# A spectral-filter and gated-MLP block, forward and backward: shift term at frequency 0, a written order of the opening's loads, sums by ones columns, and the last tile from PSUM

## Chip, cores, metric

The kernel runs on one core of one Trainium2 chip. The metric is the device time of one execution in microseconds (us); the time of a kernel is the median of its runs. Beside the runs there is one profiled execution of the same program, whose trace is read here.

## What is computed

The reference is one transformer-like block over x of 2048 rows (S) and 576 columns (D), and the gradients of all its inputs for a given grad_out:

```python
mod = silu(c) @ w_mod                       # six rows of 576: sa, ca, ga, sb, cb, gb
h = layernorm(x) * (1 + ca) + sa
x1 = x + ga * irfft2(rfft2(h) * (w_r + 1j * w_i))
h2 = layernorm(x1) * (1 + cb) + sb
out = x1 + gb * ((h2 @ w_gate) * (h2 @ w_up)) @ w_down
```

w_gate and w_up are 576 x 4608, w_down is 4608 x 576, w_mod is 576 x 3456, c is one row. All inputs are bf16. The outputs are out_0 (the block's result) and the gradients of x (out_1), w_r and w_i (out_2, out_3), w_gate, w_up, w_down (out_4 to out_6), c (out_7) and w_mod (out_8).

## The kernel before, in words

Rows go in 16 tiles (NT) of 128. D is padded to 640 (DP) where five blocks of 128 are wanted. The stages in order of time, in the profile's microseconds:

- **Opening and s1, 0 to about 60.** On SP, one load after the other: x in pieces (`x_load`), the three thirds of w_mod that are wanted first (`mod_load` of MCA, MSA, MGB), the row table RD, the column table G1, grad_out in three pieces (gonA, gonB, gonC). PE runs useless matmuls ("warm", L305) until the first data is there. `scaled_table` (L367) makes the columns of ca with 25 tiny matmuls (`mod_cols`, "modc") and scales the table RD by 1 + ca into RDs (L373, all five slabs on DVE). `shift_rows` (L376) does the same 25 matmuls for sa, puts the result into two columns of msl (L379), multiplies with RD ("zms", L384) and writes the product's row, split in a high and a low bf16 part, into two spare rows of RDs (L385 to L387). The padding of the normed tiles n1r holds ones in the columns that meet these rows (L283), so that the row transform adds sa's transform to every row. Then `pipeline` runs three steps over the tiles: `s1_norm` (statistics by `s1_stats`, normalisation on ACT, L429, transposes "trp", L434), `s1_cols` (row transform "zp", L443, with RDs; evacuation "zt") and `s1_rows` (column step "vp", L462 and L463, with G1). Statistics are made for 1, 3, 4, 4 and 4 tiles at once. Loads from x(4:8) on wait for a DVE instruction of `scaled_table` (`issue_after(first)`). `mod_make` stores each modulation row to modb_d from SP (L340).
- **u4, s2, s3, to about 300.** Transposes of grad_out (goT, L489) and products with w_down (u4, L517) fill PE. s2 takes 19 chunks of frequencies: second column step, spectrum Xc copied by ACT, stored to xn_d, multiplied with the filter ("fm", L235), first inverse step. s3 is the inverse transform, x1, the second layernorm (n2, stored to n2_d) and h2.
- **Main loop, about 300 to 1255**: 36 blocks of 128 columns of the MLP, forward and backward.
- **Tail, 1255 to the end.** t1 (per tile: the backward of the second layernorm, sums for the modulation's gradients, first steps of the transform of the gradient), t2 (filter backward, in chunks), t3 (inverse transform, backward of the first layernorm by `norm_back`, sums, store of out_1). The down projection for out_0 (u3, L1350) is dealt out between these as filler: a fixed number of its matmuls stands in PE's order after each step, and what is left follows after t3.

The sums: a column sum over rows of gh is a product with a ones pattern (`colsum`, L971; two matmuls of 288 columns per tile and sum), and the sum over rows of gh * n is taken from the diagonals of five matmuls (`diag`, L974; 4 of 128 columns and one of 64). All of a stage's tiles add up in one PSUM bank or two, opened and closed by products with zeros (`add_zero`, L966, 512 columns each). `diag_rows` (L981) masks the diagonal on DVE, `of_rows` and `of_sums` turn the sums into rows with 288-column fp32 matmuls ("spp", L991), and `section` (L1000) copies them (dmb, L1003, two buffers), writes one sixth of out_8 and adds to out_7 by products on DVE ("pr", L1016). `filter_grad` (L1188, "gwt") makes the gradients of the filter, whose spectrum Xn it loads on POOL; `store_grads` (L1322) writes them from POOL. The last half tile of out_0 goes from PSUM by ACT to a bf16 tile (L1353), then on DVE a product with gb (L1360) and a sum with x1 (L1361), then a store from POOL (L1362).

What sets the order: a scheduler orders each engine's instructions when the program is built; `in_order(list)` pins the order of the instructions given, `issue_after` and `behind` put a wait or an order behind others, `pipeline` interleaves the steps of successive tiles. At run time each engine works through its own order and waits at the first instruction that isn't ready. SP and POOL issue DMA in such an order too.

Of the kernel before, what the change touches and what calls it, by code (L numbers as in the profile page):

```python
# [9 lines left out]
FP32 = mybir.dt.float32  # L10
# [12 lines left out]
DP = 640  # L23
DF = 289
# [74 lines left out]
def build(ctx, tc, A_x, A_w_r, A_w_i, B_w_gate, B_w_up, B_w_down, c_in, w_mod, grad_out,  # L99
# [27 lines left out]
    n2_d = dram("n2_d", [128, NT, D], BF)  # L127
# [14 lines left out]
    pick = glob.tile([128, 2, 128], BF, name="pick")  # L142
    nc.vector.memset(pick[:], 0.0)
    for q in range(2):
        nc.vector.memset(pick[:, q, 64 * q:64 * q + 64], 1.0)


# [114 lines left out]
    with ExitStack() as hs:  # L262
# [18 lines left out]
        for n_ in n1r:  # L281
            nc.gpsimd.memset(n_[:, :, D:DP], 0.0)
            nc.gpsimd.memset(n_[:, :, D:DP:32], 1.0)  # L283
        RDs = hw2.tile([128, 5, 2, FP], BF, name="RDs", bufs=1)
        nc.gpsimd.memset(RDs[64:128, 4], 0.0)
        msl = hw2.tile([128, 5, 128], BF, name="msl", bufs=1)
# [9 lines left out]

        with tc.high_priority(60), nc.allow_non_contiguous_dma(reason="tiny c load"):
            c_bf = hp1.tile([128, 5], BF, name="c_bf")
            nc.vector.memset(c_bf[:], 0.0)
            nc.sync.dma_start(c_bf[:, 0:4], c_in[0, 0:512].rearrange("(m q) -> q m", q=128))  # L300
            nc.sync.dma_start(c_bf[64:128, 4:5], c_in[0, 512:576].rearrange("(m q) -> q m", q=64))
# [26 lines left out]
        def mod_make(j, wm, eng="v"):  # L328
# [11 lines left out]
            return nc.sync.dma_start(modb_d[:, j, :], modh[j][:]).ins  # L340
# [12 lines left out]
        wms = {}  # L353
        x_load(0, 1)
        wms[MCA] = mod_load(MCA)
        wms[MSA] = mod_load(MSA)
        T = {"RD": load_table(hp1, "RD", "tA")}
        x_load(1, 4)
        T["G1"] = hp1.tile(TABS["G1"], BF, name="T_G1", tag="tB")

        def g1_load(t0, t1):
            nc.sync.dma_start(T["G1"][:, t0:t1].rearrange("p a b c -> p (a b c)"), tab_d["G1"][:, t0 * 384:t1 * 384])

        g1_load(0, 4)
        opca_c = hp1.tile([128, 5], FP32, name="opca_c")

        def scaled_table():  # L367
# [3 lines left out]
            for m in range(5):  # L371
                r = slice(0, min(128, D - 128 * m))
                nc.vector.tensor_scalar(out=RDs[r, m].rearrange("p c f -> p (c f)"), in0=T["RD"][r, m].rearrange("p c f -> p (c f)"), scalar1=opca_c[r, m:m + 1], scalar2=None, op0=MUL)  # L373
            return one.ins

        def shift_rows():  # L376
            ps, parts = mod_cols(wms[MSA])
            for r, k in parts:
                nc.vector.tensor_copy(msl[r, k, 64:128:32], ps[r, k].unsqueeze(2).to_broadcast([r.stop, k.stop - k.start, 2]))  # L379
            hi = hp1.tile([128, 2, FP], BF, name="hi")  # L380
            for cc in range(2):
# [3 lines left out]
                nc.scalar.copy(RDs[64:65, 4, cc, :], zp[64:65, :FP])  # L385
                nc.vector.tensor_copy(hi[96:97, cc, :], zp[96:97, :FP])
                nc.vector.tensor_tensor(out=RDs[96:97, 4, cc, :], in0=zp[96:97, :FP], in1=hi[96:97, cc, :], op=SUB)  # L387
# [3 lines left out]
        def s1_stats(t):  # L391
            n = 1 if t == 0 else 4 - t % 4
# [14 lines left out]
        with tc.issue_after(first):  # L407
            x_load(4, 8)
            g1_load(4, NT)
            wms[MGB] = mod_load(MGB)  # L410
            for t0, t1, g in gons:
                nc.sync.dma_start(g[:, 0:(t1 - t0) * D].rearrange("p (t d) -> p t d", d=D), go_v[:, t0:t1, :])
            x_load(8, 12)
            T["BD2"] = load_table(hp1, "BD2")
            T["BDA"] = load_table(hp1, "BDA")

# [4 lines left out]
        def s1_norm(t):  # L421
            c4, tt = t // 4, t % 4
            if t == 4:
                with tc.issue_after(first):
                    x_load(12, NT)
            if tt == (1 if c4 == 0 else 0):
                s1_stats(t)
# [40 lines left out]
        mark1 = traced()  # L468
        shift_rows()
        dve0 += on_dve(mark1)[0:2]  # L470
# [4 lines left out]
        in_order(dve0 + on_dve(mark)[0:9])  # L475
# [4 lines left out]
        with tc.issue_after(first):  # L480
            nc.sync.dma_start(wn[:, 0, :, 0:DF], wr_v)
            nc.sync.dma_start(wn[:, 1, :, 0:DF], wi_v)
# [8 lines left out]
        FB4 = 2  # L491
        TWICE = 20
        turns, stored, wdTs, sts, u4_done, u4r = [], [], {}, {}, [0], []

        def u4_group(g, eng=None):
            fb, sb4 = g // 4, g % 4
            k, j = fb // FB4, fb % FB4
            if g % (4 * FB4) == 0:
                wdTs[k] = (u4w if not u4r or k % 5 < 2 else u4r[0]).tile([128, FB4, 5, 128], BF, name="wdT")
                wdn = wdn2[:, k % 2, :, :]  # L500
                with tc.issue_after(first):
                    rows = B_w_down[fb * 128:(fb + FB4) * 128, :].rearrange("(j f) d -> f j d", f=128)
                    nc.sync.dma_start(wdn[:, :, 0:D], rows)
                    nc.sync.dma_start(wdn[:, :, D:DP], rows[:, :, 512:D])
                turns.append(nc.sync.dma_start_transpose(out=wdTs[k][:].rearrange("q j m f -> q (j m) f"), in_=wdn.rearrange("f j d -> f (j d)")).ins)
# [24 lines left out]
        with ExitStack() as rc:  # L530
# [16 lines left out]
            def s2_filter(ci):  # L547
# [4 lines left out]
                X = c2.tile([128, 2, NT, 16], BF, name="Xc", bufs=3)  # L552
                if ng < 4:
                    nc.gpsimd.memset(X[:], 0.0)
                evac(X[:].rearrange("k c a m -> k (c a) m")[:, :, 0:w].rearrange("k e (j f) -> k j e f", f=4), xp[:, 0:ng, :].rearrange("k j (e f) -> k j e f", f=4), eng="a")
                nc.sync.dma_start(xn_d[:, ci * 512:(ci + 1) * 512], X[:].rearrange("k c a f -> k (c a f)"))
# [42 lines left out]

        uts, ybs, h2_made = {}, {}, []  # L600
# [19 lines left out]
        def s3_norm(sa):  # L620
# [5 lines left out]
            n2 = hw2.tile([128, 2, D], BF, name="n2")  # L626
# [6 lines left out]
            for i in range(2):  # L633
                nc.scalar.activation(out=n2[:, i, :], in_=x1[:, i, :], func=ACT.Identity, bias=nmr2[:, i:i + 1], scale=rstd2g[:, s0 + i:s0 + i + 1])
                nm = hw2.tile([128, D], BF, name="nm")
                nc.vector.tensor_tensor(out=nm[:], in0=n2[:, i, :], in1=modh[MCB][:], op=MUL)
# [238 lines left out]
    with ExitStack() as ts:  # L875
# [44 lines left out]
        sel = tl.tile([128, 2, 128], FP32, name="sel")  # L920
# [11 lines left out]
        def norm_back(pool, gn, n, rstd, res, out, name):  # L932
# [4 lines left out]
            nc.vector.scalar_tensor_tensor(out=w[:], in0=gn[:], scalar=rstd, in1=n, op0=MUL, op1=MUL, accum_out=s12[:, 1:2])  # L937
# [3 lines left out]
            if name == "1":  # L941
                nc.scalar.activation(out=w[:], in_=n, func=ACT.Identity, bias=ab[:, 0:1], scale=ab[:, 1:2])
            else:
                nc.vector.tensor_scalar(out=w[:], in0=n, scalar1=ab[:, 1:2], scalar2=ab[:, 0:1], op0=MUL, op1=ADD)
# [21 lines left out]
        def add_zero(*banks, first):  # L966

            for cs in banks:
                nc.tensor.matmul(cs[:], lhsT=ident[:], rhs=zero[:], start=first, stop=not first)

        def colsum(cs, h, src):  # L971
            nc.tensor.matmul(cs[:, 0:288], lhsT=pick[:, h, :], rhs=src, start=False, stop=False)

        def diag(cs, cs4, off, a, b):  # L974

            for m in range(5):
                o = cs[:, wide(m)] if m < 4 else cs4[:, off:off + 64]
                w = 128 if m < 4 else 64
                nc.tensor.matmul(o, lhsT=a[:, wide(m)] if m < 4 else a[:, D - 128:D], rhs=b[:, m * 128:m * 128 + w], start=False, stop=False)

        def diag_rows(pool, cs, cs4, off, name):  # L981
# [462 lines left out]
```

## Time and profile before

| | |
|---|---|
| median of 3 runs | 1522.07 us (1521.61 to 1528.6) |
| profiled execution | 1523.45 us |
| its span in the trace | 1521.7 us |
| PE busy | 1495.4 us (98%) |
| DVE busy | 1048.5 us (69%) |
| ACT busy | 580.3 us (38%) |
| POOL busy | 241.0 us (16%) |
| mean granted PE clock | 0.993 |

Engines: PE is the matmul engine (TensorE; PEld its weight loads), DVE the vector engine, ACT the scalar engine, POOL is GpSimd, SP is SyncE, which here only issues DMA (SPq is its queue). In the timeline a row is: start, duration, engine, line, operation, output<-input, shape, count, and in brackets the idle time just before it with the instruction or DMA that ended that time. Durations of matmuls overlap, so their pace is read from the starts. In groups, the columns behind the bar are total busy time, mean in ns, and idle time before with its main cause. In the windows, each engine's busy time is followed by the granted PE clock, the share of the DMA engines' time and GB/s.

### The profile page before, as it was taken

To read this page: it belongs to the slowest core of one execution; us is meant where nothing else is said; L and a number is where in the kernel's file an instruction comes from. 1 tells how busy PE (TensorE), PEld (TensorE's weight loads), DVE (VectorE), ACT (ScalarE), POOL (GpSimd) and SP (SyncE) were. 2 spreads that over 40 slices of the span, in tenths; PEclk is the share of its full clock that TensorE was granted. 3 is DMA by queue.
4 is the path that set the end of the run, shared out by engine and by line. 5 is a ranking of instruction groups with operands and counts; after the bars stand their busy time and mean duration, and the time that the engine had idled before them with its cause. 6 is when DMAs were issued, how large, how long until landed. Compare 5 with 4: busy or idle time off the path is not lost. (4 is left out here: it accounts for less than half of the span.)

```text
span 1521.7 us, 29239 instructions
## 1 busy us (share of the span) xinstructions
PE 1495.4 (98%) x11260; PEld 1020.0 (67%) x11264; DVE 1048.5 (69%) x2620; ACT 580.3 (38%) x1182; POOL 241.0 (16%) x368
## 2 busy tenths in 40 slices
PE   7999999999999999999999999999999999999998
PEld 5666643566667666666676666666766767788866
DVE  6666843667767667677676676776776777688884
ACT  5767842322222222222222222222222226586763
POOL 1101212101111111111120110110210113221022
PEclk8999999999999999999999999999999999999999
DMA  9988996688868679578688587677777779965687
GB/s 315 277 227 222 270 255 202 148 164 164 170 122 176 141 128 192 119 151 157 136 156 164 126 164 147 143 158 141 155 146 140 151 180 241 298 212 185 186 286 198
DMA packets 489470, 278.26 MB, mean 183 GB/s; under 512 B 410769, under 2 KB 461074, under 8 KB 488306
## 3 DMA queue, kind: packets, MB, share of 16 engines
q1 hardware_dynamic: 461170, 173.14, 53.5%
q0 software_dynamic: 28160, 103.25, 23.0%
q8 instruction: 88, 1.44, 0.4%
q14 instruction: 52, 0.43, 0.1%
HBM read 106.59 MB, written 82.16 MB: 124 GB/s over the span
## 5 line engine op out<-in xcount | busy, mean ns | idle before, releaser
L816 DVE TENSOR_TENSOR acc<-acc,u8p 128x288 f32<-128x288 f32 (+1 forms) x1088 | 482.9, 452 | 276.2 <-PE u8p L811 272.7
L811 PE MATMUL u8p<-wT,ggT 128*128 128x288 bf16 x1152 | 327.9, 286 | 1.6 <-DVE acc L816 1.6
L811 PE MATMUL u8p<-wT,guT 128*128 128x288 bf16 x1152 | 327.6, 286 | 0.0
L775 PE MATMUL gup<-h2T,wgu 128*128 128x512 bf16 x1152 | 297.8, 379 | 0.0
L710 ACT CAST so<-u57p 128x288 bf16<-128x288 f32 x216 | 86.2, 399 | 532.6 <-PE u57p L708 527.3
L708 PE MATMUL u57p<-h2p,gu_sf 128*128 128x288 bf16 x1152 | 186.4, 286 | 0.0
L708 PE MATMUL u57p<-h2p,gg_sf 128*128 128x288 bf16 x1152 | 185.9, 286 | 0.0
L775 PEld LDWEIGHTS <-wgu 128*128 128x128 bf16 x1152 | 109.6, 98 | 97.9 <-issue 16.6
L811 PEld LDWEIGHTS <-ggT 128*128 128x128 bf16 x1152 | 112.6, 98 | 66.5 <-issue 14.0
L517 PE MATMUL u4p<-goT,wdT 128*128 128x512 bf16 x656 | 151.9, 379 | 0.0
L811 PEld LDWEIGHTS <-guT 128*128 128x128 bf16 x1152 | 112.7, 98 | 57.6 <-issue 2.4
L1350 PE MATMUL u3p<-wd,hl 128*128 128x288 bf16 x936 | 142.4, 289 | 0.0
L777 ACT CAST gT<-gup 128x512 bf16<-128x512 f32 x144 | 84.4, 586 | 131.8 <-PE gup L775 129.9
L708 PEld LDWEIGHTS <-hh_sf 128*128 128x128 bf16 x1152 | 112.7, 98 | 28.4
L708 PEld LDWEIGHTS <-gu_sf 128*128 128x128 bf16 x1152 | 112.4, 98 | 28.5
L708 PEld LDWEIGHTS <-gg_sf 128*128 128x128 bf16 x1152 | 112.4, 98 | 28.2
L1350 PEld LDWEIGHTS <-hl 128*128 128x128 bf16 x1152 | 108.4, 99 | 26.0 <-issue 0.3
L777 ACT CAST uT<-gup 128x512 bf16<-128x512 f32 x144 | 84.4, 586 | 77.5 <-PE gup L775 77.5
L517 PEld LDWEIGHTS <-wdT 128*128 128x128 bf16 x656 | 61.3, 98 | 71.1 <-issue 7.3
L708 PE MATMUL u57p<-gonC,hh_sf 128*128 128x288 bf16 x576 | 99.7, 286 | 0.0
L788 POOL DMA_DIRECT2D hhT_d<-hhT x36 | 33.3, 925 | 376.3 <-DVE hhT L779 333.5
L173 DVE CAST ghh_st<-u4p 128x512 bf16<-128x512 f32 x56 | 38.6, 690 | 58.7 <-PE u4p L517 57.3
(389 smaller groups left out, 1864.9 us busy)
## 6 DMA issues: line engine op xcount, KB each, us to landing
ghhT_d<-ghh_st POOLq DMA_DIRECT2D x36, 512.0 KB, 4.3
ghh<-ghhT_d POOLq DMA_DIRECT2D x36, 512.0 KB, 7.7
hhT_d<-hhT POOLq DMA_DIRECT2D x36, 512.0 KB, 6.5
hl<-hhT_d SPq DMA_DIRECT2D x28, 576.0 KB, 5.7
out_dram<-woT SPq DMA_DIRECT2D x70, 128.0 KB, 2.0
wdn<-in_B_w_down_dram SPq DMA_DIRECT2D x18, 288.0 KB, 4.4
wd<-in_B_w_down_dram POOLq DMA_DIRECT2D x36, 144.0 KB, 4.3
out_dram<-so SPq DMA_DIRECT2D x36, 144.0 KB, 2.4
```

The lines of the kernel that those rows point to most:

```text
L173: nc.vector.tensor_copy(dst, src)
L517: nc.tensor.matmul(pt[:], lhsT=wdTs[k][:, j, m, :], rhs=goT[:, 4 * sb4:4 * sb4 + 4, m, :], start=(m == 0 and n == 5), stop=(m == n - 1))
L708: mm = nc.tensor.matmul(pw[0][:, 0:288], lhsT=sf[:, t, :], rhs=rhs_n(t, h * 288, 288), start=(t == 0), stop=(t == NT - 1))
L710: followed(mm, nc.scalar.copy(so[:, h * 288:(h + 1) * 288], pw[0][:, 0:288]))
L775: nc.tensor.matmul(pts[k][:], lhsT=wgu[:, 4 * wi_ + m, jw * 128:(jw + 1) * 128], rhs=h2T[:, ts_, m, :], start=False, stop=(m == 3))
L777: nc.scalar.copy((gT, uT)[wi_][:, th_, :], pts[k][:])
L788: nc.gpsimd.dma_start(hhT_d[:, :, fb, :].rearrange("tp f x -> f tp x"), hhT[:].rearrange("f (tp ti) p -> f tp (ti p)", ti=2))
L811: nc.tensor.matmul(pu[:, 0:288], lhsT=l_, rhs=r_, start=(k == 0), stop=(k == len(mms) - 1))
L816: summed[t] = nc.vector.tensor_tensor(out=ghb(t)[:, hs_] if fbs[-1] == NFB - 1 else dst, in0=dst, in1=pu[:, 0:288], op=ADD).ins
L1350: mm = nc.tensor.matmul(p2[ti][:, 0:288], lhsT=hls[fb // 9][:, fb % 9, ti * 128:(ti + 1) * 128], rhs=w[:, fb - f0, h * 288:(h + 1) * 288], ...
```

## The change

1. **Shift term.** `shift_rows` becomes `shift_row`, called after s1's pipeline: it loads sa's third of w_mod there, makes its columns and the ten zms matmuls there, and ACT copies the one row, times S, to a small fp32 tile sz. sa is the same for each row of x, so its transform over the rows lies at frequency 0 alone: in each chunk of s2 DVE adds sz to partition 0 of the spectrum before it is stored and multiplied. The ones in n1r's padding go.
2. **Opening.** All opening loads up to the first two transposes of w_down stand in a written order on SP (x(0), MCA, RD, x(1:4), G1, x(4:8), G1, MGB, grad_out and w_down in turn with x); the wait for `first` goes. The table BD2 and the two c loads are issued ahead of x(0). Stores to modb_d go from POOL. RDs' fifth slab is scaled by ACT. Statistics are taken for 1, 1, 2, 2, 2, 4 and 4 tiles.
3. **Sums.** n2 and n1 are kept in rows of six blocks of 96 with two ones behind each (spacing 98; written by ACT through a strided view, n1c loaded by a strided DMA of 192-byte pieces). `diag` is six matmuls of 97 columns, of which the last gives the plain sum; for the sum with yc, six of 96. `colsum`, `sel`, `pick` and the closing zero products go. `diag_sums` copies the six columns, and `of_sums` spreads them with three small DVE products of 96 columns per half ("dx", one buffer).
4. **Last tile.** The ACT copy of the last half is dropped; DVE takes product and sum in halves, the second half's product from PSUM.
5. **Stores of the filter's gradients** come 6, 6 and 4 behind tiles 11, 12 and 13, before 4 each behind tiles 11 to 14.

On the engines' orders as built: PE has 11233 matmuls, before 11254; the order of its fillers between t1's, t2's and t3's steps is the same; the sections' spp matmuls after t3 stand some fillers later or earlier; DVE has the first two sections' dx products between the last filter gradients.

```diff
-            for m in range(5):
-                r = slice(0, min(128, D - 128 * m))
-                nc.vector.tensor_scalar(out=RDs[r, m].rearrange("p c f -> p (c f)"), in0=T["RD"][r, m].rearrange("p c f -> p (c f)"), scalar1=opca_c[r, m:m + 1], scalar2=None, op0=MUL)
+                dst, src = (x[r, m].rearrange("p c f -> p (c f)") for x in (RDs, T["RD"]))
+                if m == 4:
+                    nc.scalar.activation(out=dst, in_=src, func=ACT.Copy, scale=opca_c[r, m:m + 1])
...
-        def shift_rows():
-            ps, parts = mod_cols(wms[MSA])
+        def shift_row():
+            wm = mod_load(MSA)
+            ps, parts = mod_cols(wm)
             for r, k in parts:
-                nc.vector.tensor_copy(msl[r, k, 64:128:32], ps[r, k].unsqueeze(2).to_broadcast([r.stop, k.stop - k.start, 2]))
-            hi = hp1.tile([128, 2, FP], BF, name="hi")
+                nc.vector.tensor_copy(msl[r, k, 0:1], ps[r, k].unsqueeze(2))
...
-                nc.scalar.copy(RDs[64:65, 4, cc, :], zp[64:65, :FP])
-                nc.vector.tensor_copy(hi[96:97, cc, :], zp[96:97, :FP])
-                nc.vector.tensor_tensor(out=RDs[96:97, 4, cc, :], in0=zp[96:97, :FP], in1=hi[96:97, cc, :], op=SUB)
+                nc.scalar.activation(out=sz[0:1, cc, :], in_=zp[0:1, :FP], func=ACT.Copy, scale=float(S))
...
-            n = 1 if t == 0 else 4 - t % 4
+            n = 1 if t < 2 else 2 if t < 8 else 4
...
+                nc.vector.tensor_tensor(out=x0, in0=p0, in1=z0, op=ADD)
                 nc.sync.dma_start(xn_d[:, ci * 512:(ci + 1) * 512], X[:].rearrange("k c a f -> k (c a f)"))
...
-            for m in range(5):
-                o = cs[:, wide(m)] if m < 4 else cs4[:, off:off + 64]
-                w = 128 if m < 4 else 64
-                nc.tensor.matmul(o, lhsT=a[:, wide(m)] if m < 4 else a[:, D - 128:D], rhs=b[:, m * 128:m * 128 + w], start=False, stop=False)
+            for m in range(6):
+                o = cs[:, m * w:m * w + w] if m < 5 else cs6[:, off:off + w]
+                c0 = m * DC if m < 5 else D - 128
+                nc.tensor.matmul(o, lhsT=a[:, c0:c0 + 128], rhs=b[:, m * step:m * step + w], start=False, stop=last_ and m >= 4 and (m == 4 or shut))
...
+                x = secp.tile([128, 288], FP32, name="dx", bufs=1)
+                for m in range(3 * h, 3 * h + 3):
+                    mask = ident[:, 0:DC] if m < 5 else ident[:, 128 - DC:128]
+                    nc.vector.tensor_scalar(out=x[:, m % 3 * DC:m % 3 * DC + DC], in0=mask, scalar1=d[:, m:m + 1], scalar2=None, op0=MUL)
+                return spread(ones_f[:], x[:])
...
+                        for hs_, src in ((slice(0, 288), obs[ti][:, 0:288]), (slice(288, D), p2[ti][:, 0:288])):
+                            nc.vector.tensor_tensor(out=of[:, hs_], in0=src, in1=gb_h[:, hs_], op=MUL)
+                            nc.vector.tensor_tensor(out=of[:, hs_], in0=of[:, hs_], in1=x1t[:, ti, hs_], op=ADD)
...
-                    if 11 <= t < 15:
-                        for k in range(4 * (t - 11), 4 * (t - 10)):
-                            store_grads(k, stored.ins)
+                    for k in {11: range(6), 12: range(6, 12), 13: range(12, NT)}.get(t, ()):
+                        store_grads(k, stored.ins)
```

## The prediction, made blind

> **What bounds the kernel now.** I read first the busy time by windows, to see in which stage the matmul engine (PE) stands still; then the waits of PE, for who holds it up there; then the timeline of single engines around each wait.
>
> ```profile
> core 0: us, PE busy (x) PEld busy (x) DVE busy (x) ACT busy (x) POOL busy (x), PEclk, DMA share, GB/s
> 10.00:20.00 10.00, 4.87 (x25) 2.56 (x24) 6.39 (x20) 1.36 (x5) 0.00 (x0) 0.78 1.05 407
> 60.00:260.00 200.00, 199.89 (x1318) 108.98 (x1317) 117.16 (x316) 117.80 (x233) 37.33 (x67) 1.00 0.87 237
> ```
>
> ```profile
> PE csC L979 <- DMA yc<-y_d: 2.9, 1, 2.9
> PE trp L434 <- ACT n1r L429: 2.8, 1, 2.8
> PE spp L991 <- ACT dmb L1003: 2.7, 1, 2.7
> PE zp L443 <- DVE RDs L387: 2.7, 2, 2.1
> PE zms L384 <- DVE msl L379: 2.3, 1, 2.3
> ```
>
> The columns of the second view are total wait, times and longest. From 60 to 260 us PE is busy 199.89 of 200 us: there only PE work counts. Of the five large waits three (trp, zp, zms) lie in the opening, one (csC) in the tail's first stage t1, one (spp) near the end. So a part of the change is worth time if it shortens one of these waits or takes work from PE where PE does not wait.
>
> **Part 1 and 2: shift term and opening order.** The opening before:
>
> ```profile
> 12.44 2.61 PE L384 MATMUL zms<-T_RD,msl 128*128 128x292 bf16 x10 [2.25 <-DVE msl L379]
> 14.85 1.05 PE L443 MATMUL zp<-RDs,hT 128*128 128x292 bf16 x4
> 17.99 0.80 PE L443 MATMUL zp<-RDs,hT 128*128 128x292 bf16 x5 [2.09 <-DVE RDs L387]
> ...
> 22.60 0.71 PE L434 MATMUL trp<-ident,n1r 128*128 128x128 bf16 x5 [2.81 <-ACT n1r L429]
> ...
> 27.87 0.89 PE L347 MATMUL modc<-sc_bf,wm 128*128 128x1 bf16 x25
> ```
>
> ```profile
> 3.46 0.43 SPq L324 DMA_DIRECT2D wm<-in_w_mod_dram  x1
> 3.93 0.51 SPq L325 DMA_DIRECT2D wm<-in_w_mod_dram  x1
> 4.48 0.51 SPq L242 DMA_DIRECT2D T_RD<-tab_RD  x1
> ```
>
> ```profile
> 10.79 1.49 DVE L373 TENSOR_SCALAR RDs<-T_RD,opca_c 128x584 bf16<-128x584 bf16 x5 [2.69 <-DMA T_RD<-tab_RD]
> ...
> 13.46 0.82 DVE L183 BATCH_NORM_STATS2 ln_st<-h2p 128x6 f32<-128x288 bf16 x2 [1.03 <-DMA h2p<-in_A_x_dram]
> ```
>
> ```profile
> 6.58 0.87 ACT L429 ACTIVATE n1r<-h2p,ln_nmr,rstd1g 128x576 bf16<-128x576 bf16 x1 [0.42 <-DVE ln_nmr L188]
> 8.28 0.69 ACT L171 COPY hT<-trp 128x640 bf16<-128x640 bf16 x1 [0.83 <-PE trp L434]
> ```
>
> The first tile's row transform zp (14.85 to 18.8 and on) is broken twice because its table RDs gets the two shift rows from L385-387, and the second tile's transposes (22.60) come late because the statistics of tiles 1-3 share DVE with those copies. Removed here: the load of the shift columns of w_mod (issued 3.46 and 3.93, 576 + 144 KB) ahead of RD, 25 modc and 10 zms matmuls, two msl and four one-row DVE copies, two ACT copies. Added ahead of x(0): the small table BD2 and both c loads, three issues of about 0.5 like those of 3.46 to 4.48, so x(0) comes about 1.5 us later.
>
> Step by step: 720 KB at the window's 407 GB/s are 1.8 us, so RD lands at 10.79 - 1.8 = 9.0. Four scalings on DVE at 1.49/5 = 0.30 (the fifth goes to ACT) end at 10.2; the first tile's normed transpose hT, before at 8.28 + 0.69 = 9.0, is there at about 10.5 through x(0)'s delay. So zp(0) starts at about 10.5, not 14.85, and nothing breaks it. x(1:4) lands at 13.46 - 1.8 = 11.6. Only one tile is now taken at once: statistics 0.82, aggregation, square root and two small operations together about 1 (an estimate), then the normalisation of 0.87: trp(1) at about 14.3 instead of 22.60, **-8.3**. The 35 matmuls come back at the end of the stage, where PE is full: 0.89 + 10 x 0.122 (the 288-column spacing of t1, below) = **+2.1**. The half clock stays as it is in my sum, since PE would again stand from about 11.8 to 14.3. Net **-6.2**. Ends: -11, if nearly all opening waits go and the clock holds; -1.8, if only the transfer that was removed counts and the next transfer (G1, x(4:8), grad_out) is late in its place. The middle is nearer to the rows, since nothing that zp(0) and trp(1) need lies behind other loads now.
>
> What hides the rest: the shift load is issued behind two DMA transposes on SP, and its matmuls stand among the last ones of the stage, some 40 us after the start; the modb_d stores go to POOL, which is idle there. In the filter stage 19 small DVE adds stand between the spectrum's copy and its products. The nearest row is a one-row DVE operation of 0.47 (L387's kind); 19 of them are 8.9 us if nothing covered them. The u4 matmuls do: PE was busy 199.89 of 200 while DVE had 117 busy. I take 0, ends 0 and +8.9.
>
> **Part 3: plain sums by ones columns.** In t1, per tile:
>
> ```profile
> 1260.89 0.41 PE L972 MATMUL csB<-acc,pick 128*128 128x288 bf16 x2
> 1261.13 0.39 PE L979 MATMUL csA<-n2c,acc 128*128 128x128 bf16 x4
> 1261.36 0.19 PE L979 MATMUL csB<-n2c,acc 128*128 128x64 bf16 x1
> 1261.38 0.39 PE L979 MATMUL csC<-yc,gxr 128*128 128x128 bf16 x4
> ...
> 1261.64 1.51 PE L708 MATMUL u57p<-h2p,gg_sf 128*128 128x288 bf16 x11
> ```
>
> Starts are what count (ends overlap). 288 columns take 0.122 (11 of them from 1261.64 on, and two 0.24), 128 take 0.23/4 = 0.056, 64 about 0.025, so 97 or 96 columns about 0.043. The group takes 1261.64 - 1260.89 = 0.75 now and 12 x 0.043 = 0.51 then: 0.24 less a tile, 16 tiles 3.8, and three closing matmuls of 512 columns (4 x 0.056 each) 0.65. But the 2.9 us wait for yc comes after eight tiles, and the loads before it run on SP without a gap:
>
> ```profile
> 1283.32 4.66 SPq L1039 DMA_DIRECT2D n2c<-n_d  x1
> ...
> 1295.45 0.32 SPq L1039 DMA_DIRECT2D yc<-y_d  x1
> ```
>
> So that wait ends when SP's chain of transposes ends, not when PE arrives. I let the end of the wait move by the first three tiles only (0.7; SP still waits for PE there, an estimate), the eight tiles behind it give 8 x 0.24 = 1.9, the closing ones 0.65: **-3.2**. Ends 0 and -4.5.
>
> [...] The rows above, each with new weights, show 56 ns at 128 columns, and the 25 modc matmuls of one column each, all with new weights, 36 ns; the measurement decides here.
>
> In t3 the same 0.24 comes off:
>
> ```profile
> 1403.79 0.41 PE L972 MATMUL csE<-ghr,pick 128*128 128x288 bf16 x2
> ...
> 1404.29 0.78 PE L1350 MATMUL u3p<-wd,hl 128*128 128x288 bf16 x5
> ```
>
> ```profile
> L937 DVE SCALAR_TENSOR_TENSOR w<-gn,rstd1g,n1c 128x576 bf16<-128x576 bf16 x16 | 13.1, 819 | 0.6
> L1188 DVE SCALAR_TENSOR_TENSOR gwt<-Xn,b_Vp 128x512 f32<-128x512 bf16 x18 | 11.7, 687 | 3.7 <-DMA Xn<-xn_d 3.5
> ...
> L945 DVE TENSOR_TENSOR ob<-u,w 128x576 bf16<-128x576 bf16 x16 | 7.3, 457 | 7.9 <-ACT w L942 7.9
> ```
>
> But here DVE's loop (gn, w, ab, u, ob, ghr) waits for nothing but ACT's w, in 0.5 us pieces, 7.9 in all: DVE and ACT close a circle that PE is no part of, and the colsums start in the moment that ghr ends. PE would only wait instead. I take **-0.4** of 3.8 + 0.43; ends 0 and -4.3. The strided views of 96 of 98 in w cost nothing in my sum: the broadcast view of L1188 takes 687/512 = 1.34 ns an element, the plain one of L937 819/576 = 1.42.
>
> **The late wait.** After t3:
>
> ```profile
> 1463.66 1.29 DVE L1188 SCALAR_TENSOR_TENSOR gwt<-Xn,b_Vp 128x512 f32<-128x512 bf16 x2 [3.45 <-DMA Xn<-xn_d]
> ...
> 1473.21 0.08 DVE L1016 DVE_READ_ACCUMULATOR pr<-wmj,dmb 64x1 f32 x1
> ```
>
> ```profile
> 1473.78 1.33 PE L991 MATMUL spp<-dgb,ones_f 128*128 128x288 f32 x2 [2.72 <-ACT dmb L1003]
> ```
>
> ```profile
> 1473.00:1480.00 7.00, 6.22 (x24) 3.88 (x25) 5.97 (x17) 6.56 (x12) 0.67 (x2) 0.51 0.77 238
> ```
>
> PE waits until DVE has done the first section's products, which stand behind filter gradients that wait for a load. The change puts twelve small DVE operations in (nine of them before these products, some in the gap before the load) and takes the same PE work out ahead of the wait. The wait's end stays where it is, PE comes earlier, and half a clock follows as now: **0**, ends -5 (wait and half clock gone) and +3.
>
> **Part 4 and 5: last tile and stores.**
>
> ```profile
> 1514.80 0.40 ACT L1353 CAST ob<-u3q 128x288 bf16<-128x288 f32 x1 [4.01 <-PE u3q L1350]
> ```
>
> ```profile
> 1515.23 0.46 DVE L1360 TENSOR_TENSOR of<-ob,gb_h 128x576 bf16<-128x576 bf16 x1
> 1515.72 0.46 DVE L1361 TENSOR_TENSOR of<-of,x1t 128x576 bf16<-128x576 bf16 x1
> ```
>
> ```profile
> L816 DVE TENSOR_TENSOR acc<-acc,u8p 128x288 f32<-128x288 f32 (+1 forms) x1088 | 482.9, 452 | 276.2 <-PE u8p L811 272.7
> ```
>
> The chain is 0.40 + 0.46 + 0.46 with hops, 1514.80 to 1516.18. Then it is one product from PSUM (L816's kind, 0.45) and a half sum (under 0.46, I take 0.30): 1515.6, so 0.6 less. Six wn stores no longer run beside the last tile's: 0.2. **-0.8**, ends 0 and -2.
>
> **The sum.** -6.2 - 3.2 - 0.4 + 0 - 0.8 = -10.6, against the profiled execution of 1523.45 (span 1521.7): 1512.9. The median of the three runs is 1522.07, 1.4 lower, so I forecast **1512**.
>
> **The rivals.**
> A: t3 does pay, its loop having a little slack through PE after all, and the late wait shrinks with it: 4 more, about **1507.5**. For it: PE has no recorded wait in t3. Against: the colsums start as ghr ends, 16 times.
> B: the opening is bound by transfers (407 GB/s, DMA share 1.05 in the window): the wait moves from RD to x or G1 and only 1.8 is won: **1516.5**. Against: PE waited for RDs, msl and n1r, each behind DVE and not behind DMA.
> C: t1 gives nothing, because SP's loads follow their own pace throughout or because narrow matmuls have a floor: **1515**. For it: the gapless SP chain.
> D, slower: t3's circle of DVE and ACT gets longer through the strided views (w on DVE 0.82, on ACT 0.87), paid 16 times with no cover. Break-even is 10.6/16 = 0.66 a tile; at half the rate it would be 1.69 a tile, +27, that is **1539**. Against: L1188's row. That the change does not do what it says is B's and C's form: work moved, wait kept.
>
> **How the numbers follow.** Forecast (1508 to 1516) 0.50, A 0.14, B 0.17, C 0.12, D 0.05, others 0.02. The range takes the forecast, the better part of A, and B and C with their scatter: 1504 to 1519. A measurement of this kernel can tell about 0.5%, 7.6 us, from no change: below 1514.5 is faster. From the forecast 0.46, A 0.14 and half of C 0.05: 0.65 faster; the rest of the forecast, of C, and B: 0.28 same; D and half of the others 0.07 slower.
>
> **What would show it.** Right: zp(0) in one piece at 10 to 11 us and trp(1) at 14 to 15; no L387; t1's group at 0.51 with the csC wait longer than 2.9; t3's period still about 3.75 with PE now waiting for ghr; spp's wait still ending when the first section's products do; 1.4 less ACT and DVE work behind the last matmul. Wrong: trp(1) after 18 us, or new waits for h2p, T_G or gonA; DVE's w above 0.9 us in t3; a PE wait on Xc or fm between 60 and 260.

## The result, and the profile after

The changed kernel takes 1513.54 us (median of 20 runs, 1509.13 to 1524.16), the kernel before 1521.83 us (median of 20 runs, 1519.58 to 1528.6). The ratio is 0.9949, with a 95% interval of 0.9934 to 0.9965: 8 us less, a gain at about the size that a measurement of this kernel can tell from none. The forecast was 1512, and 1504 to 1519. The profiled execution of the changed kernel took 1517.03 us, its span is 1515.3, which is 6.4 less than the 1521.7 of before. It is one of the slower executions (15th of the 20), and the experiments show why.

The waits of the matmul engine (PE) in the changed kernel, in total, times and longest; those under 0.7 us are left out at the end:

```profile
PE u3p L1380 <- DMA hl<-hhT_d: 2.8, 2, 2.3
PE spp L1023 <- DVE dx L1034: 2.2, 2, 1.8
PE u3p L1380 <- DMA wd<-in_B_w_down_dram: 1.9, 1, 1.9
PE trp L458 <- ACT n1r L453: 1.8, 1, 1.8
PE u8p L834 <- DVE acc L839: 1.6, 2, 1.3
PE warm L311 <- POOL ident masks.py:199: 1.6, 1, 1.6
PE modps L338 <- DMA wm<-in_w_mod_dram: 1.4, 1, 1.4
PE zp L1116 <- ACT b_Vp L1125: 1.2, 7, 0.2
PE zp L467 <- ACT hT L176: 1.2, 2, 0.9
PE upb L219 <- ACT ye L1311: 1.2, 2, 0.8
PE vp L487 <- ACT zt L176: 1.0, 2, 0.6
PE csD L999 <- DVE ghr L1312: 0.7, 1, 0.7
PE modc L353 <- DMA wm<-in_w_mod_dram: 0.7, 1, 0.7
```

All five waits that the prediction started from are gone or, for trp, 1 us shorter (zms, the two of zp for RDs, csC for yc, spp for dmb in its old length). In their place stand waits of 0.5 to 2.3 us for DMA (hl, wd, wm) and for dx. So the change does what it says, and the question is what the new waits cost.

Four landmarks that exist in both programs cut the span into parts. M is the last wait in the main loop (u8p for acc), T is the start of t3's last diagonal matmul, G is the start of the closing gcp product, behind the last filler, E is the end.

| | M | T | G | E |
|---|---|---|---|---|
| before | 1251.36 | 1450.37 | 1514.60 | 1521.7 |
| changed | 1249.31 | 1443.33 | 1509.45 | 1515.3 |
| difference of the part that ends here | -2.05 | -4.99 | +1.89 | -1.25 |

(M to T was 199.01 and is 194.02, T to G 64.23 and 66.12, G to E 7.10 and 5.85; the four add up to -6.4.) The forecast had -6.2 for the first part, -3.6 for the second, 0 for the third and -0.8 for the last.

**The opening.** The timeline of PE in the changed kernel:

```profile
10.95 1.42 PE L467 MATMUL zp<-RDs,hT 128*128 128x292 bf16 x10 [0.89 <-ACT hT L176]
14.15 0.45 PE L458 MATMUL trp<-ident,n1r 128*128 128x128 bf16 x5 [1.78 <-ACT n1r L453]
...
15.38 2.53 PE L467 MATMUL zp<-RDs,hT 128*128 128x292 bf16 x10 [0.28 <-ACT hT L176]
19.27 1.14 PE L338 MATMUL modps<-wm,sc_rep 128*128 128x288 bf16 x4 [1.35 <-DMA wm<-in_w_mod_dram]
```

The first tile's row transform is in one piece at 10.95 (forecast 10.5), the second tile's transposes at 14.15 (14.3): 8.45 earlier than the 22.60 of before. Then the lead melts: the third tile's transposes start at 22.80 instead of 28.83 (-6.0), the fourth's at 26.51 instead of 31.36 (-4.85), the last's at 59.28 instead of 63.83 (-4.55). The windows say where it went; the column behind POOL is the granted clock of PE:

```profile
12.00:15.50 3.50, 1.43 (x13) 0.75 (x12) 3.50 (x15) 2.52 (x6) 0.69 (x1) 1.00 1.02 412
15.50:26.00 10.50, 9.15 (x70) 6.24 (x69) 4.29 (x18) 5.19 (x10) 1.32 (x2) 0.51 1.07 397
26.00:33.00 7.00, 6.55 (x66) 4.98 (x64) 6.03 (x21) 6.22 (x15) 0.55 (x1) 1.00 1.15 284
```

From 15.5 to 26.0 PE has half a clock (0.51), and it is busy there, 9.15 of 10.5 us. The second tile's zp above takes 2.53 where the first took 1.42. Before the change half clocks lay at 12.2 to 15.6 and at 19.1 to 25.9, and in the second of these stretches PE was busy only 3.7 of 6.8 us. Ahead of the main loop the 35 moved matmuls come back (62.84 to 65.56 in the trace, with three others of 0.65 in all between them), as forecast 2.1, and -4.55 becomes about -2.

**t1 and t3.** One tile's group in t1:

```profile
1263.34 0.39 PE L999 MATMUL csA<-n2c,acc 128*128 128x97 bf16 x5
1263.57 0.21 PE L999 MATMUL csB<-n2c,acc 128*128 128x97 bf16 x1
1263.61 0.37 PE L999 MATMUL csC<-yc,gxr 128*128 128x96 bf16 x5
1263.82 0.21 PE L999 MATMUL csB<-yc,gxr 128*128 128x96 bf16 x1
1263.86 1.02 PE L731 MATMUL u57p<-h2p,gg_sf 128*128 128x288 bf16 x7
```

It takes 1263.86 - 1263.34 = 0.52 for 0.75 (forecast 0.51), twelve pairs of weight load and matmul at 43 ns each; before, four pairs at 128 columns took 0.23 us. In t3 the 15 steps from the first to the last diagonal group take 56.86 instead of 57.39 (1392.51 to 1449.90): half a microsecond for 3.6 us of PE work less, as forecast.

**The late tail.** PE from t3 to the last filler, its waits and the first dgb product:

```profile
1451.56 0.75 PE L1023 MATMUL spp<-dx,ones_f 128*128 128x288 f32 x2 [1.78 <-DVE dx L1034]
...
1458.49 0.75 PE L1023 MATMUL spp<-dga,ones_f 128*128 128x288 f32 x2 [0.49 <-ACT dmb L1042]
...
1466.43 1.13 PE L1023 MATMUL spp<-dgb,ones_f 128*128 128x288 f32 x4
...
1493.44 2.33 PE L1380 MATMUL u3p<-wd,hl 128*128 128x288 bf16 x9 [2.27 <-DMA hl<-hhT_d]
1495.56 5.23 PE L1380 MATMUL u3q<-wd,hl 128*128 128x288 bf16 x36
```

The product of dgb, where before a wait of 2.72 ended 23.4 behind T, starts 23.1 behind T without a wait: PE has waited for dx and dmb earlier, 1.78 and 0.49 us, and no half clock followed there. The 2.27 for hl is new, and there the half clock came: 9 matmuls of u3p in 2.12 (1493.44 to 1495.56) instead of 1.10, and 36 of u3q in 5.07 instead of 4.41.

**The end.** The last tile in the changed kernel, on DVE and POOL:

```profile
1509.65 0.46 DVE L1397 TENSOR_TENSOR of<-u3q,gb_h 128x288 bf16<-128x288 f32 x1 [1.15 <-PE u3q L1380]
...
1510.15 0.29 DVE L1398 TENSOR_TENSOR of<-of,x1t 128x288 bf16<-128x288 bf16 x1
```

From the gcp product to the end of the last sum it is 1510.44 - 1509.45 = 0.99, before 1516.18 - 1514.60 = 1.58: the forecast's 0.6.

### The profile page after: what moved, and what is told of

It reads as the page before. It is cut to its first block, busy times and chain, and to the rows that moved or that the text cites. A ratio compares the mean times of both kernels' runs of the same rounds, so it can differ in the third digit from the quotient of the medians.

```text
span 1515.3 us, 29225 instructions
## 1 busy us (share of the span) xinstructions
PE 1489.1 (98%) x11243; PEld 1013.2 (67%) x11243; DVE 1050.8 (69%) x2651; ACT 581.1 (38%) x1184; POOL 243.2 (16%) x376
## 4 chain that ended last, share of the span: by engine, by line
PE 87%; DMA 5%; DVE 3%; issue 2%; ACT 2%; SPq 0%; POOL 0%; POOLq 0%; DVEq 0%
PE u57p L731 27%; PE u8p L834 18%; PE gup L798 17%; PE u4p L534 9%; PE u3p L1380 3%; PE gup L793 3%; DMA wmj<-in_w_mod_dram 2%; PE yp L223 1%; PE zp L467 1%; DMA wm<-in_w_mod_dram 1%; ACT w L965 1%; DVE w L960 1%; DMA wd<-in_B_w_down_dram 1%; PE u4p L529 1%; PE upa L217 1%
```

## Experiments

**Theory.** The sums give 4 to 5 us of PE work in t1 and 0.5 in t3; the opening's gain is cut by a half clock whose place changes from execution to execution and by the wait for MGB's load; the new wait for hl comes from the filter gradients' stores, which now go 6, 6 and 4. **Rivals:** the opening is bound by its transfers; t1's gain is due to another phase of the queues; hl is late through the sections' own transfers.

### The sums alone

The kernel before with part 3 of the change (sums, ones columns, no closing zeros) and nothing else.

> The kernel before with the change to the sums alone (part 3); opening, shift term, last tile and stores as before. Theory: t1's group shrinks from 0.75 to 0.52, so t1 gains about 3.7 from its PE work plus what the yc wait gives (2.9 before); t3's period stays at 3.8 because DVE and ACT set it (total gain over t3's 16 tiles under 0.8); the end of t3 stands 4.5 to 5.5 earlier than in the kernel before, the opening is unchanged (last wait in the main loop at 1251.4). Rival: the gain in t1 came from the other phase of the DMA queues that the earlier opening gave; then the yc wait of about 2.9 is back here and grows, and t1 gains 2 or less.

Measured: 1515.92 median, ratio 0.9970 (0.9956 to 0.9983). M 1251.41, T 1446.68, G 1507.97, E 1514.4. The opening is that of before, and T is 3.7 earlier, not the 4.5 to 5.5 expected, because waits for DMA add up to 3.39 between M and T:

```profile
PE u3p L1365 <- DMA wd<-in_B_w_down_dram: 2.4, 1, 2.4
...
PE csC L984 <- DMA yc<-y_d: 1.0, 1, 1.0
```

Without its DMA waits M to T is 195.27 - 3.39 = 191.88, against 199.01 - 2.91 = 196.10 before. The wait for yc fell to 1.0, so it isn't the fixed thing for which the forecast took it, nor did it grow as the rival said.

### The opening alone

The kernel before with parts 1 and 2 (shift term and opening; sz in bf16 for want of room); its sums as before.

> The kernel before with the shift term and the opening of the changed kernel alone (sz in bf16 for want of room, pick and sums as before). Theory: the main loop ends 1 to 4.7 earlier than at 1251.4, by where the half clock falls; t1's group stays 0.75 and its wait for yc comes back at 2.9 or more, the late wait for dmb with its half clock is there as before; in all 1 to 4 less than the kernel before. Rival: the sums are needed for the opening's gain to last, since t1's waits for transfers take it back: 0 to 1.

Measured: 1519.69 median, ratio 0.9980 (0.9965 to 0.9995). M 1248.00, T 1444.13, G 1506.70, E 1514.3. M is 3.4 earlier. There is no wait for yc or wd at all in this execution, against the expectation, and M to T is 196.13, just what the old sums take without their waits (196.10). The late wait is there as before:

```profile
PE spp L1006 <- ACT dmb L1018: 2.4, 1, 2.4
```

The two ratios, 0.0030 and 0.0020 below 1, add up to 0.0050; the whole change measured 0.0051.

### MGB's load first, and useless work in PE's waits

```diff
+        wms[MGB] = mod_load(MGB)
         x_load(4, 8)
         g1_load(4, NT)
-        wms[MGB] = mod_load(MGB)
```

> The changed kernel with the load of MGB put ahead of x(4:8) and the rest of G1; nothing else moves. Theory: the opening lost 1.35 to the wait of modps for this load and some 2.3 more to a half clock that stays from 15.5 to 25.9 because PE waits again there; with the load early the modps wait goes, the clock comes back one window (3.4) earlier at best, and the main loop ends 1.3 to 3 us earlier than at 1249.3. Rival: the opening is bound by the sum of the transfers; then as much waiting turns up at h2p, T_G or gonA, and the main loop ends at the same time.

> As the run before it, with 28 useless matmuls of 128 columns put behind the first tile's row transform, so that PE is busy where it would wait for the second tile. Theory: no half clock in 15 to 26 us (or one window less), so the main loop ends 3 to 5 us earlier than at 1249.3, and the spread of the runs gets smaller. Rival: the half clock comes anyway (the fill is 1.6 us of a wait of 1.8), and the 28 matmuls, if they are late, cost up to 1.6.

> As the run with MGB ahead and 28 useless matmuls behind the first tile's row transform, with 24 more ahead of the second tile's, so that PE has work in both of its waits between 12 and 18 us. Theory: what the opening gains hangs on when the half clock comes; the same opening ended the main loop at 1246.8 to 1250.2 in five profiles. With both waits filled there is no half clock before 26 us and the main loop ends at 1244.5 to 1246.5. Rival: the half clock comes from the waits before 11 us or in spite of the fill; then 1247 or later.

The second and third add, behind the first tile's row transform and (the third) ahead of the second tile's:

```diff
+        for _ in range(28):
+            nc.tensor.matmul(warm2[:, 0:128], lhsT=ident[:], rhs=ident[:], start=True, stop=True)
...
+            if t == 1:
+                for _ in range(24):
+                    nc.tensor.matmul(warm3[:, 0:128], lhsT=ident[:], rhs=ident[:], start=True, stop=True)
```

Measured: ratios 0.9947 (0.9932 to 0.9961), 0.9943 (0.9928 to 0.9958) and 0.9951 (0.9932 to 0.9971), M at 1247.31, 1247.43 and 1247.66. The wait of modps is gone in all three, and the wait of zp for the second tile's hT grew instead, from 0.28 to 0.69, 2.14 and 0.93. PE starts MGB's modulation no earlier for it, at 19.0, 19.8 and 18.9 us. So the waiting turned up elsewhere, as the rival said, but at hT, which ACT makes, and not at a load. With both fills the clock stays whole, for the only time in these openings:

```profile
10.00:20.00 10.00, 7.97 (x94) 6.46 (x92) 7.36 (x30) 6.73 (x14) 0.85 (x2) 1.00 1.05 402
20.00:30.00 10.00, 8.50 (x105) 6.52 (x103) 7.59 (x29) 8.26 (x18) 1.92 (x3) 1.00 1.06 391
```

Yet M is 1247.66 and not under 1246.5: with a whole clock PE has waits of 0.5 to 1.4 us for ACT and DMA in the opening. So work in PE's waits went with a whole clock in this one execution, but gave nothing at M. That the chain of statistics and normalisation on DVE and ACT took it back is argued from these waits and not shown. None of the three beats the changed kernel.

### The changed kernel once more

> The changed kernel once more, for a second profile. Theory: end of the main loop between 1246.7 and 1250.2, by the clock in 12 to 26 us; t3 from first to last group 56.9; from there to the last matmul 60.5 to 62 with a wait for hl under 2, or 66 if a half clock follows it. Rival: the first profile's 1249.3 and 66.1 come again, being the kernel's own.

Measured: M 1249.40, T 1446.01, G 1508.98, E 1514.9, 1516.72 us. M and the wait for hl (2.26) came as in the first profile, but no half clock followed this time (62.97 from T to G, 66.12 in the first). One came in t1 instead, behind a wait of 2.33 for wd.

The traces show why the same wait is followed by a half clock in one execution and not in the other. In these traces the clock changes in steps of 3.41 us only. These are the windows between such steps in which the wait for hl ended, each with the next one, in the first profile and then in the second:

```profile
1490.07:1493.48 3.41, 1.14 (x10) 0.69 (x9) 0.00 (x0) 1.80 (x3) 0.00 (x0) 1.00 1.16 181
1493.48:1496.89 3.41, 3.41 (x15) 2.11 (x16) 0.00 (x0) 0.40 (x1) 0.00 (x0) 0.50 1.03 256
```

```profile
1490.71:1494.12 3.41, 1.66 (x14) 1.08 (x12) 0.00 (x0) 2.37 (x4) 0.00 (x0) 1.00 1.15 242
1494.12:1497.53 3.41, 2.89 (x24) 2.33 (x25) 0.00 (x0) 0.40 (x1) 0.00 (x0) 1.00 1.07 222
```

In the second the wait falls across two windows, and PE is busy 1.66 us in the first of them and not 1.14. Counted over all 14 traces to the end of PE's work, and with the one-column modc matmuls left out of PE's busy time, 24 windows at full clock have 1.51 us of PE work or less, and a half clock follows each of them; 6088 have 1.58 us or more, and none is followed by one. Of the windows at half clock, 12 have 2.76 us or less, and the half clock stays for the next window; 24 have 2.95 or more, and it ends. So in these traces PE's work in a window decides, and not the longest wait. (With modc counted as work there are five exceptions, all windows that hold modc's 25 matmuls. The count was made afterwards, and no run was made to test it.)

Eight profiles have the changed kernel's opening as it is. This is their half clock ahead of and behind 19 us, worked out from the granted clock of the windows 9 to 19 and 19 to 30 us (2 x length x (1 - clock)), and M:

| half clock before 19 us | half clock behind 19 us | M, us |
|---|---|---|
| 3.4, 3.0 | 6.8, 7.3 | 1249.31, 1250.20 |
| 0 | 6.8 | 1248.92, 1249.12, 1249.40 |
| 3.4 | 0 | 1246.76, 1247.66, 1248.00 |
| 3.4, opening of before | 6.8 | 1251.36, 1251.41 |

One of those with none behind 19 us (the run with 16 stores below), and then the second profile:

```profile
10.00:20.00 10.00, 6.95 (x46) 4.32 (x45) 8.14 (x31) 7.42 (x15) 1.41 (x2) 0.87 1.05 401
20.00:30.00 10.00, 9.12 (x113) 7.19 (x111) 7.69 (x27) 8.18 (x19) 0.71 (x3) 1.00 1.06 393
```

```profile
10.00:20.00 10.00, 4.62 (x35) 2.85 (x34) 7.66 (x30) 6.71 (x14) 1.47 (x2) 0.98 1.05 401
20.00:30.00 10.00, 10.00 (x101) 7.90 (x100) 5.29 (x20) 6.00 (x13) 0.55 (x1) 0.68 1.09 393
```

The line is drawn at 19 us because the load of MGB lands at 18.8 to 19.3 in all eight, and PE starts its modulation at 18.9 to 19.3, whatever it did before. A half clock ahead of that only shortens the wait for the load (0.8 to 1.4 us against 2.0 to 2.4) and costs next to nothing at M (1249.31 and 1250.20 with it, 1248.92 to 1249.40 without). The half clock behind it, two windows long (in the first profile 18.92 to 25.75; the first of the two has, beside MGB's modc matmuls, 2.58 us of PE work), costs about 2 us: M is 1249.4 in the mean of the five that have it and 1247.5 in the three that don't.

### More PE work in t3

```diff
+            if sa < NT - 1:
+                nc.tensor.matmul(csE[:], lhsT=ident[:], rhs=zero[:], start=False, stop=False)
```

> The changed kernel with one product with zeros of 512 columns (0.216 us of PE) more after each of t3's first 15 diagonal groups, 3.2 us of PE work in all, nearly what the change took out of t3. Theory: DVE and ACT set t3's pace, so from the first to the last diagonal group (1385.87 to 1442.73 in the changed kernel, 56.9) it stays under 57.7. Rival: PE had become the one that waits only a little; then the stage grows by 2 to 3.2.

Measured: first group 1386.91, last 1443.81, 56.90. The 3.2 us of extra work cost 0.04. The last group, in this kernel and then in the changed one; the wait only got shorter:

```profile
1443.81 0.26 PE L999 MATMUL csD<-n1c,ghr 128*128 128x97 bf16 x2 [0.48 <-DVE ghr L1312]
```

```profile
1442.73 0.26 PE L999 MATMUL csD<-n1c,ghr 128*128 128x97 bf16 x2 [0.70 <-DVE ghr L1312]
```

So t3's pace is set by DVE and ACT, as the forecast had it, and rival A falls.

### dx in a tile of its own

```diff
-        tl.tile([128, 816], FP32, name="gap_l")
+        dxs = tl.tile([128, 816], FP32, name="gap_l")
...
-                x = secp.tile([128, 288], FP32, name="dx", bufs=1)
+                x = dxs[:, h * 288:(h + 1) * 288]
```

> The changed kernel with the dx products in a tile of their own, two halves, in place of one buffer in memory that t3's tiles held before. Theory: PE's waits for dx (1.8 + 0.5 in the changed kernel's trace) come from that memory: DVE waits for the store of out_1's last tiles before it may write there, and for the one buffer; they go. The end of the first section's products moves little, so the last matmul comes 0 to 1.5 earlier. Rival: dx is late because DVE is busy with filter gradients; the waits stay over 1.

Measured: M 1247.66, T 1445.70, G 1508.46, E 1514.7. The wait for dx falls to 0.3, and the old wait for dmb comes back at dgb's product:

```profile
1468.67 0.75 PE L1023 MATMUL spp<-dgb,ones_f 128*128 128x288 f32 x2 [1.65 <-ACT dmb L1042]
```

It ends 23.0 behind T, near where it ends with the old sums (23.4 before, 23.1 with the opening alone). In the profiles with the one buffer there is no wait here, and the product starts 21.8 to 23.1 behind T. So the waits for dx and for dmb stand in for each other; that one moment on DVE sets both is not shown. It was not isolated whether memory or the single buffer made dx late.

### The gradients' stores: 4 each, 16 at once, none

```diff
-                    for k in {11: range(6), 12: range(6, 12), 13: range(12, NT)}.get(t, ()):
+                    if 11 <= t < 15:
+                        for k in range(4 * (t - 11), 4 * (t - 10)):
...
```

> The changed kernel with the filter gradient's stores 4 each behind tiles 11 to 14, as before the change. Theory: the new wait for hl at 1493 (2.3 us and the half clock behind it, some 3.5 in all) comes from 12 stores of 144.5 KB that share the DMA engines with that load (it took 14.7 to landing); with 4 each the load lands in time, the wait is gone or under 0.5, and the last matmul comes 2 to 3.5 us earlier than 1509.5; behind it the end may take 0.5 to 1.2 longer. Rival: the load is late because of the sections' own transfers (o, wmj) on SP; then the wait stays at 1.5 or more.

For the next two the line reads `for k in range(NT) if t == 11 else ():` and `... if t == 15 else ():`.

> The changed kernel with all 16 stores of the filter's gradients behind tile 11 (2.3 MB at once) in place of 6, 6 and 4. Theory: these stores are what delays the load of hl behind them; the wait for hl in the late tail is 2.3 or longer (3 to 7), mostly with a half clock behind it. Rival: the sections' own transfers delay it; then the wait stays between 0 and 2.3.

> The changed kernel with all 16 stores of the filter's gradients behind the last tile, so that no such store runs beside the late loads of hl; the end behind the last matmul gets 2 to 6 longer by them. Theory: the stores hold up hl; without them the slowest hl load lands in under 12 (13.3 to 17.6 in eight profiles with the stores in 6, 6 and 4, or all at once; 11.2 to 13.5 in five with 4 each), there is no wait for hl in the late tail, and from t3's last diagonal group to the last matmul it is 60 to 61. Rival: the sections' own transfers hold it up; then the slowest load stays at 13 or more.

Measured: with 4 each ratio 0.9956 (0.9939 to 0.9972), G 1502.87, no wait for hl behind T. With 16 at once G 1506.12, E 1513.0, no wait for hl behind T either, which misses what the theory expected. With none beside hl: ratio 1.0026 (1.0009 to 1.0043), G 1507.17, E 1530.1, no wait for hl over 0.3, T to G 60.30, the shortest of all. Its waits in t1 were long (3.2 for yc, and a half clock), but they lie ahead of any of these stores. From issue to landing, the two late loads of hl in the changed kernel and then with the stores last:

```profile
DMA to landing us min/median/max: 13.3/14.7/16.1
```

```profile
DMA to landing us min/median/max: 5.9/6.2/6.5
```

The slowest load of hl behind 1440 took 8.8 us to land without such stores, 11.2 to 13.5 in five profiles with 4 each (never a wait for it over 0.6 in the late tail), 14.4 with 16 at once, 13.3 to 17.6 in seven profiles with 6, 6 and 4, where five had a wait of 1.3 to 3.5. So the stores do slow the load, which is shown by taking them away. How long a wait comes of it differs from execution to execution, and the count of stores alone doesn't order it. Put behind the last tile they make G to E 22.97 instead of 5.85:

```profile
1508.99 10.71 POOL L1352 DMA_DIRECT2D out_dram<-wn  x15
```

### The three mends together

MGB's load first, 4 stores each and dx in its own tile, in the changed kernel.

> The changed kernel with MGB's load ahead of x(4:8), the gradients' stores 4 each as before, and dx in its own tile. Theory: the opening's 2 us, the hl wait's 2 to 3 and dx's 0 to 1.5 add up but for what t1's waits for transfers take back (2 us of the first run with MGB ahead): 1508 to 1511 in the median, 0.9920 to 0.9945 of the kernel before. Rival: the waits of t1 and the late tail only change places; 1512 to 1514.

Measured: 1513.31 median, ratio 0.9954 (0.9941 to 0.9968). M 1248.06, T 1441.78, G 1502.36, E 1509.6 in its profile, but in the runs no better than the changed kernel: the rival's case. No version was found that is clearly faster than the changed kernel.

## Why the prediction was right or wrong

**The opening: two steps failed, "the half clock stays as it is in my sum" and the lead of the second tile taken for the lead of the whole stage.** The moments of zp(0) and trp(1) came within 0.5 us of the working, and so did the price of the 35 moved matmuls. But the gain was not 6.2; it was 1.2 to 4.6 over eight profiles, 2.7 in the mean (M 1248.67 against 1251.38). First, the half clock at 19 to 26 us is there before the change and in five of the eight. Before, PE was busy 3.7 of its 6.8 us; now it is busy in nearly all of it (6.48 of 6.83 in the profile of the result), and these five end about 2 us later than the other three. Second, even those three gain 3.4 to 4.6: of the lead of 8.45 at the second tile's transposes 5.9 to 7.1 are left at the last tile's (57.95, 56.75 and 56.71 against 63.83). The forecast looked at what zp(0) and trp(1) need and not at the next instruction in PE's order: MGB's modulation stands ahead of the third tile and waits 0.8 to 2.4 us for its load. With that load first and a whole clock M was 1247.66 all the same, so the load is not the only bound; what the next one is stays open. Rival B, at 0.17, had this in its outcome (a gain of 1.8 from the opening). A wait for a load did come, at MGB and not at x or G1, but taking it away gave nothing clear.

**t1: right in the group's price, wrong about the wait.** 0.24 a tile was forecast, 0.23 measured. That "the wait ends when SP's chain ends", so that the first eight tiles give only 0.7, fell: the waits for DMA between M and T are not the program's but the execution's. With the old sums they were 2.91 and 0, with the new ones 0.61 to 4.76. With the waits taken out, M to T is 196.10 and 196.13 with the old sums and 191.61 to 191.88 with the new, in the seven profiles without a half clock in t1: 4.4 us for the sums, of which t3 has 0.5. Rival C falls with it.

**t3: right**, -0.5 for -0.4, and the reason held when 3.2 us of work were put back at a price of 0.04. Rival D needed a longer w on DVE; w takes 817 ns after and 819 before, so the strided views are free.

**The late wait: its price was wrong.** What failed is "PE comes earlier, and half a clock follows as now": the wait was cut into pieces at dx and dmb, and in no profile with the new sums did a half clock come at this place. Without a wait for hl, T to G was 60.3 to 61.3 in six profiles (62.2 in a seventh, with 1.2 for gcd), against 64.2 before, so the term is about -3 and not 0. This is so although more work stands there: the four products for dsb, 1.3 us, were in t3 before, where PE has time, and come behind T now (24 spp products, before 20). Rival A had the late wait shrink with t3; it shrank without it. In the profiled execution the hl wait and its half clock took 2.27 + 1.0 + 0.7 = 4.0 back. The prediction counted the moved stores only by what they save at the end and didn't ask what they run beside.

**The end: right.** 0.6 by the shorter chain; G to E was 7.1, 6.4 and 7.6 with the old end and 5.8 to 6.9 with the new (seven profiles, 6.1 in the mean): -0.9 for -0.8. How it divides is less clear: with the new last tile and 4 stores each it was 6.8 and 7.3 (4 stores each alone, and the three mends), no better than before, so the stores weigh more than the 0.2 forecast for them.

So the total came near by luck, through errors of opposite sign: some 3.5 too much in the opening, some 3 too little in the late tail and some 0.8 too little in t1 and t3; the slower load of hl took part of that back. The 19 small adds in the filter stage cost nothing, as taken: PE was busy 199.93 of 200 us from 60 to 260.

What stays open is why the DMA waits in t1 differ so much between executions of the same program; they were seen, not varied. That they and the half clocks make the changed kernel's wide spread (1509 to 1524) fits the profiles, but the single runs have no trace to show it.

## What to carry to other kernels

Price a wait that goes by what the engine will do in that time: here a half clock cost next to nothing at M where PE had to wait for a load anyway (ahead of 19 us) and about 2 us where the gap was filled (behind it), so read the granted clock beside the waits. After the first instruction that is freed, walk on through the engine's own order until one is found that still waits (here MGB's modulation, 0.8 to 2.4 us for its load). And a moved DMA has two prices, its own end and the load that it now runs beside (here a load of hl that took up to 16.1 us to landing, and 6.5 without the stores).

## What the runs showed of the hardware that was not expected

- The half clock of PE came in pieces of 3.41 us, in the opening at 0, 1, 2 or 3 pieces for nearly the same program. With the one-column modc matmuls left out, it followed each of the 24 full-clock windows of that length with 1.51 us of PE work or less, and none of the 6088 with 1.58 us or more; it stayed behind half-clock windows with up to 2.76 us and ended behind those with 2.95 or more. The longest wait did not decide: waits of 2.27 and 2.26 us for the same load left PE busy 1.14 us in one window and 1.66 in the other, and only the first was followed by it.
- Beside six stores of 144.5 KB and again six, a 576 KB load took 16.1 us to landing; with the stores moved away it took 6.5.
- A view of six blocks of 96 in 98 costs DVE nothing in a product with accumulation: 817 ns against 819 for the plain one.
